# Linear attention and two channel mixers on one core: four weight clamps moved to GpSimd, bonus sums and low parts of four tiles moved to TensorE

## The chip, the cores and the metric

The kernel runs on one core of a Trainium2 chip. The metric is device time in microseconds (us), the median over runs. Trace times count from the first instruction of one profiled execution. The engines are named as in the profile: PE (TensorE matmul), PEld (its weight load), DVE (VectorE), ACT (ScalarE), POOL (GpSimd), SP (SyncE, which issues the DMAs).

## The reference

Three layers follow each other. All inputs and outputs are float32.

```python
# 1. linear attention with decay, batch 4, 8 heads, 768 steps, head size 48
for t in range(S):
    cur = einsum('bhd,bhe->bhde', u * k[t], v[t])
    y[t] = einsum('bhd,bhde->bhe', r[t], state + cur)
    state = w * state + einsum('bhd,bhe->bhde', k[t], v[t])
# 2. x = y as [4, 768, 384]; gated mixer with a 3-tap convolution along the sequence
h = relu(x @ w_in)                      # 384 -> 1024
c = conv3(h, conv_w);  x1 = (h * sigmoid(c)) @ w_out
# 3. residual mixer
out = x1 + relu(layernorm(x1) * g_ln @ w_ch1) @ w_ch2   # 384 -> 1536 -> 384
```

The term with `u` is the bonus: for one position and head it is the sum over the head's 48 entries of r·u·k, times v.

## The kernel before, in words

**Tiles.** The sequence is cut into tiles of 128 positions: 24 tiles (`NT`), 6 per batch entry. Attention works tile by tile. Within a tile the decayed r and k (`rk`, transposed, scaled in place by the tables `trk`) give a score matrix per head (`dot_products`, eight matmuls into two PSUM tiles `dps`); its strict upper triangle, with the bonus on the diagonal, is `aT`; `products` multiplies `aT` with v and adds the contribution of the carried state (`sbd`), into the PSUM tile `yps`. The state is carried by `state_sum` (PE, from the scaled keys `kks`, into PSUM `pst`) and `state_update` (DVE and ACT).

**Split numbers.** Matmuls of the mixers take each float32 operand as a high part (`xh`, rounded to fp32r by an ACT copy) and a low part (`xl`, the rest), and add three products: high·high, high·low, low·high (`mm3`, `down`). The weights are split on the chip as well: 22 weight jobs (`wjob`), each of which loads a block, takes |w| on ACT, clamps it (`magnitude`), decodes it with a shift and two bit operations on DVE (`decode`), rounds the high part on ACT and subtracts on DVE for the low part. Jobs 0 to 9 are `w_in` and `w_out`, which the first mixer needs; jobs 0 to 2 and 4 to 6 are 512 wide, the others 768. The clamp of a job is issued one job ahead (`ahead`), just behind the second bit operation of the job before.

**Three kinds of tiles.** Tiles 0 to 3 (`EARLY`) run in `startup`, ahead of all mixer work, in an order written out by hand and interleaved with weight jobs (`wdo`). Tiles 0 to 5 (`LIGHT`) go through `light_tile`: the bonus sums come from PE (z = scaled r times scaled k on DVE, four matmuls with the small matrix `ub` into `pa8`, an ACT copy to `a8`), are multiplied with v on POOL (`va`) and added by PE. Tiles 4 and 5 also take the low part from PE: `yps` minus `xh` by one matmul with a negated identity (`minus`), then an ACT copy. Tiles 6 to 23 use the other form: the bonus from the untransposed k and r by a multiply (`av`) and a reduce on DVE (`a8`), eight ACT activations that write diagonals into `aT`, two predicated copies on DVE that put the scores above the diagonal, and the low part by a DVE subtract straight after the high part. For this form the keys are scaled with two tables at once (`decayed_k`, 768 wide: decay and bonus); the light form scales with one (384 wide).

**Order.** `attention` is a generator whose steps are called from the first mixer's loop (`after1`, at slots listed in `STEPS`); each tile is itself a generator, advanced by `go_on`. In the usual round of tile n one step holds the state sum of n, its update and the first segment of tile n+1 (scaling, bonus); the next holds products of n and then the scores of n+1. PE runs strictly in the order written. On DVE, ACT, POOL and SP the instructions issued through `vo`, `ao`, `go` and `so` are kept behind the instruction written just before them on that engine, and all others are placed by a planner that simulates the program. In `startup` everything on these engines goes through the ordered forms, so that each engine runs it exactly as written. All attention PSUM tiles with tag `pa` (`dps`, `pa8`, `yps`, `pst`) share three buffers; a tile that finds none free waits for a reader to finish.

The change touches `magnitude`'s caller, `load_rows`, `decayed_k`, `attn_tile`, `startup` and `attention`.

Of the kernel before, what the change touches and what calls it, by code (L numbers as in the profile page):

```python
# [8 lines left out]
F32 = mybir.dt.float32  # L9
F32R = mybir.dt.float32r  # L10
I32 = mybir.dt.int32
AF = mybir.ActivationFunctionType
ALU = mybir.AluOpType
AX = mybir.AxisListType

B, H, S, D = 4, 8, 768, 48
DM = H * D
# [5 lines left out]
C = 128  # L23
# [9 lines left out]
NP = H // 2  # L33
PR = 112
# [2 lines left out]
EARLY = 4  # L37
HAND = 9
LIGHT = 6
STEPS = (2, 4, 6, 8, 10, 12, 15), (1, 3, 4, 6, 7, 9, 10, 12, 14, 16)  # L40
GC = 16
GE = 4
# [8 lines left out]
def body(ctx, tc, r, k, v, w, u, w_in, conv_w, w_out, g_ln, w_ch1, w_ch2, rkT, krv, small, out):  # L51
    nc = tc.nc
# [4 lines left out]
    ap = ctx.enter_context(tc.tile_pool(name="ap", bufs=2))  # L57
# [4 lines left out]
    ps_a = ctx.enter_context(tc.tile_pool(name="ps_a", bufs=3, space=PS))  # L62
    dram = ctx.enter_context(tc.tile_pool(name="dram", bufs=1, space=bass.MemoryType.DRAM))

    v_ = nc.vector
    a_ = nc.scalar
# [12 lines left out]
    pe = InOrder(nc.tensor)  # L79
    vo = InOrder(nc.vector)  # L80
    ao = InOrder(nc.scalar)
    so = InOrder(nc.sync)
    go = InOrder(nc.gpsimd)
# [3 lines left out]
    ident = tables_[:, 0:128]  # L87
    trk = tables_[0:PR, 128:128 + 2 * NP * C].rearrange("x (a p c) -> x a p c", a=2, p=NP)
    tr, tkd = trk[:, 0], trk[:, 1]
    o = 128 + 2 * NP * C  # L90
# [31 lines left out]
    def magnitude(st, n, engine=go):  # L122

        t = ap.tile([128, WN], F32, tag="wd", name="wdec", bufs=2)[:, 0:n]
        ao.activation(out=t, in_=words(st, n)[1].bitcast(F32), func=AF.Abs)
        engine.tensor_scalar(out=t, in0=t, scalar1=W_MIN, scalar2=W_MAX, op0=ALU.max, op1=ALU.min)
        return t
# [14 lines left out]
    def wjob(src, n, hi, lo, scale=None):  # L142

        st, mag = [], []

        def load():
            st.append(io.tile([128, 2 * WN], I32, tag="st" if me >= 4 else "first", name="st", bufs=3 if me >= 4 else 4))
            dst = st[0][:, 0:2 * n]
            if len(src.shape) == 3:
                dst = dst.rearrange("p (a n) -> p a n", a=src.shape[1])  # L150
            so.dma_start(out=dst, in_=src.bitcast(I32))

        def ahead():
            if not mag:
                mag.append(magnitude(st[0], n, vo if me < 10 else go))

        def steps():
            ahead()
            t = mag[0]
            yield from decode(st[0], n, t)  # L160
            if me + 1 < min(len(wjobs), w_loaded[0]):
                wjobs[me + 1][2]()
            if len(src.shape) == 3:
                t = t.rearrange("p (a n) -> p a n", a=src.shape[1])
            kw = {} if scale is None else {"scale": gl[:, scale:scale + 1]}
            ao.activation(out=hi, in_=t, func=AF.Copy, **kw)
            yield
            if scale is None:
                vo.tensor_tensor(out=lo, in0=t, in1=hi.bitcast(F32), op=ALU.subtract)
            else:  # L170
                vo.scalar_tensor_tensor(out=lo, in0=t, scalar=kw["scale"], in1=hi.bitcast(F32),
                                        op0=ALU.mult, op1=ALU.subtract)
        me = len(wjobs)
        wjobs.append((load, steps(), ahead))
        return len(wjobs) - 1

# [34 lines left out]
    def wdo(count=1, last=None):  # L211

        for _ in range(count):
            while w_done[0] < (len(wjobs) if last is None else last + 1):
                wload(w_done[0] + 3)
                if next(wjobs[w_done[0]][1], "end") != "end":
                    break
                w_done[0] += 1
# [21 lines left out]
                     rv[:, DM:].rearrange("x (h d) -> x h d", h=H), rv)  # L240

    def load_rows(n, s_, rv):
        c0 = DM if n < LIGHT else 0
        s_.dma_start(out=rv[:, c0:], in_=krv[n, :, DM + c0:])

    xT = {}
# [5 lines left out]

    def decayed_k(n):

        if n < LIGHT:
            vo.tensor_tensor(out=kks[:, n % 2, 0, :, 0:D], in0=loaded[n][1], in1=tku[:, 0], op=ALU.mult)
            return
        inputs(n).tensor_tensor(out=kks[:, n % 2, :, :, 0:D], in0=loaded[n][1].unsqueeze(1).to_broadcast([128, 2, H, D]), in1=tku,
                         op=ALU.mult)
# [29 lines left out]
    def halos(n, xh, xl):  # L289
        i, j = n % TPB, n // TT  # L290
        g_ = vo if n < EARLY else nc.gpsimd
        for t, e in ((xh, 0), (xl, 1)):
            if i == 0:
                g_.memset(t[:, :, 0:1].bitcast(F32), 0.0)
            if i == TPB - 1:
                g_.memset(t[:, :, T + 1:T + 2].bitcast(F32), 0.0)
            if n % TT == 0 and i > 0:
                g_.tensor_copy(out=xT[j - 1][e][:, :, T + 1:T + 2], in_=t[:, :, 1:2].bitcast(F32))
                g_.tensor_copy(out=t[:, :, 0:1], in_=xT[j - 1][e][:, :, T:T + 1].bitcast(F32))
# [19 lines left out]
    def light_tile(n, rk, vt, py, py_tag):  # L319
# [45 lines left out]
        finished[0] = n  # L365
        yield

    def attn_tile(n):
        b, i = divmod(n, TPB)
        rk, _, rt, vt, _ = loaded[n]  # L370
        py, py_tag = (ps_c, "acc") if n < EARLY else (ps_a, "pa")

        rT, kT = rk[:, 0], rk[:, 1]
        vo.tensor_tensor(out=rk, in0=rk, in1=trk, op=ALU.mult)
        if n < LIGHT:
            yield from light_tile(n, rk, vt, py, py_tag)
            return
        av = ap.tile([128, H, D], F32, tag="av", name="av", bufs=2)
        v_.tensor_tensor(out=av, in0=kks[:, n % 2, 1, :, 0:D], in1=rt, op=ALU.mult)
        a8 = sp.tile([128, H, 1], F32, tag="a8", name="a8", bufs=2)  # L380
        v_.tensor_reduce(out=a8.rearrange("x (q p) o -> x q (p o)", q=2), in_=av.rearrange("x (p q) d -> x q p d", q=2),
                         axis=AX.X, op=ALU.add)
        aT = ap.tile([128, 2, NP, C], F32, tag="aT", name="aT", bufs=2)
        for h in range(H):
            a_.activation(out=aT[:, h // NP, h % NP, :], in_=ident, func=AF.Copy, scale=a8[:, h, :])
        yield

        dps = dot_products(rT, kT)
        for q in range(2):
            v_.copy_predicated(out=aT[:, q], mask=later.bitcast(I32).unsqueeze(1).to_broadcast([128, NP, C]), data=dps[q])  # L390
        yield

        yps = py.tile([128, KT, C], F32, tag=py_tag, name="yps")
        products(n, yps, rT, vt, aT)
        j = n // TT
        xh, xl = xT[j] if j in xT else new_xT(j)
        sl = slice(1 + (n % TT) * C, 1 + (n % TT) * C + C)
        a_.activation(out=xh[:, :, sl], in_=yps, func=AF.Copy)
        v_.tensor_tensor(out=xl[:, :, sl], in0=yps, in1=xh[:, :, sl].bitcast(F32), op=ALU.subtract)
        load_tile(n + 3)  # L400
        if n + 2 < NT:
            decayed_k(n + 2)
        halos(n, xh, xl)
        finished[0] = n
        yield
# [3 lines left out]
    def state_sum(n):  # L409
        vt = loaded[n][3]  # L410
        if n % TPB != TPB - 1:
            pst = sums[n] = ps_a.tile([128, NP, D], F32, tag="pa", name="pst")
            for h in range(H):
                q0 = 64 * (h % 2)
                pe.matmul(pst[q0:q0 + 64, h // 2, :], lhsT=kks[:, n % 2, 0, h, :], rhs=vt[:, h, 0:D], start=True,
                          stop=True)
# [18 lines left out]
    def startup():  # L435

        tiles = {n: attn_tile(n) for n in range(EARLY + 1)}

        def on(n):
            next(tiles[n], None)  # L440

        decayed = decayed_k
        on(0), decayed(0), on(0)
        on(1), state_sum(0), state_update(0), decayed(1), on(1), state_sum(1)
        wdo(1)
        on(0), on(2), state_update(1), decayed(2)
        wdo(2)
        on(2), state_sum(2), on(0)
        wdo(1)
        on(1), on(3), state_update(2), decayed(3)  # L450
        wdo(2)
        on(3), state_sum(3), on(1)
        wdo(2)
        on(2), state_update(3)
        wdo(3)
        on(2), on(3)
        wdo(1)
        on(3)
        wdo(1)
        on(4), decayed(4)  # L460
        wdo(3)
        return tiles

    def attention(tiles):

        def go_on(n):
            if 0 <= n < NT:
                next(tiles.setdefault(n, attn_tile(n)), None)

        n = EARLY  # L470
        load_tile(n + 2)
        decayed_k(n + 1)
        go_on(n)
        yield
        for n in range(EARLY, NT):
            state_sum(n)
            state_update(n)
            go_on(n - 1)
            if n != LIGHT - 1:
                go_on(n + 1)  # L480
            yield
            go_on(n)
            if n == LIGHT - 1:
                yield
                go_on(n)
                go_on(n + 1)
                yield
            go_on(n + 1)
            yield

    def split_T(x, n, hi, lo, c0):
# [456 lines left out]
```

## Time and profile before

| | us |
|---|---|
| median of three runs | 653.33 (652.41 to 654.55) |
| the profiled execution | 653.91 |
| its span, first to last instruction | 652.2 |
| PE busy | 627.9 |
| DVE busy | 421.7 |
| ACT busy | 300.8 |
| POOL busy | 81.2 |

The profiled execution lasts 1.7 us longer than its span, and is 0.6 us above the median. Busy time is the time in which an engine had an instruction running. PE is busy nearly all the span, but its clock is not always granted in full, and DVE has its work mostly in the first half.

### The profile page before, as it was taken

The page shows a single profiled execution, that of the slowest core. Times are in us where ns is not written, and L with a number is a line of the kernel's source. Part 1 is how long each engine was busy: PE and PEld are TensorE (multiplying, and loading weights), DVE is VectorE, ACT ScalarE, POOL GpSimd, SP SyncE. Part 2 cuts the span into 40 slices and gives each one's busy share as a digit, 9 for nine tenths or more (in the row PEclk, how much of TensorE's full clock was granted, in tenths as well). Part 3 has the DMA queues.
Part 4 walks back from the last instruction along what each step waited for, and adds up shares of the span by engine and source line. Part 5 has one row for each costly group of instructions (what it writes and reads, how often), then busy time and mean ns, then how long its engine had stood idle before and what let it go on. Part 6 is the DMA issues. An engine that isn't in the chain of part 4 may idle for free.

```text
span 652.2 us, 11821 instructions
## 1 busy us (share of the span) xinstructions
PE 627.9 (96%) x4803; PEld 572.3 (88%) x4803; DVE 421.7 (65%) x793; ACT 300.8 (46%) x658; POOL 81.2 (12%) x108
## 2 busy tenths in 40 slices
PE   8969879999999999999999999999999999999996
PEld 5768868889999999999999999999999999999995
DVE  6989999999989999968978834314213422422111
ACT  3447677687687877766755511211211211211110
POOL 6312010110020001002115501001000100100000
PEclk8867989999999999999999999999999999999999
DMA  8934644444253524012125103002002001100001
GB/s 231 309 107 156 211 146 125 125 133 159 71 174 118 162 83 137 18 47 88 52 82 171 60 0 98 1 0 98 1 0 83 16 0 50 50 0 19 31 0 54
DMA packets 25296, 56.52 MB, mean 87 GB/s; under 512 B 2961, under 2 KB 15378, under 8 KB 25234
## 3 DMA queue, kind: packets, MB, share of 16 engines
q1 hardware_dynamic: 25234, 55.68, 27.1%
q8 instruction: 40, 0.66, 0.4%
q14 instruction: 22, 0.18, 0.1%
HBM read 46.24 MB, written 9.44 MB: 85 GB/s over the span
## 4 chain that ended last, share of the span: by engine, by line
PE 84%; DVE 10%; ACT 2%; issue 1%; DMA 1%; POOL 1%; SPq 0%; DVEq 0%; ACTq 0%; POOLq 0%
PE acc L77 36%; PE psm L77 36%; PE yps L77 5%; PE dps L77 4%; DVE wdec L77 3%; DVE c L541 2%; PE pst L77 2%; PE pxt L77 1%; DVE rk L77 1%; DMA x1b<-x_dram 1%; DVE c L522 1%; PE pa L77 1%; DVE gl L528 1%; DVE kks L77 0%; POOL tables L762 0%
## 5 line engine op out<-in xcount | busy, mean ns | idle before, releaser
L555 DVE SCALAR_TENSOR_TENSOR rl<-psm,rh 128x512 fp32r<-128x512 f32 x72 | 49.6, 689 | 136.0 <-ACT rh L554 132.5
L554 ACT ACTIVATE rh<-psm 128x512 fp32r<-128x512 f32 x72 | 43.1, 599 | 199.6 <-PE psm L77 199.5
L77 PE MATMUL acc<-c2h,rh 128*128 128x384 f32 x288 | 97.0, 337 | 0.0
L77 PE MATMUL acc<-c2l,rh 128*128 128x384 f32 x288 | 97.0, 337 | 0.0
L77 PE MATMUL acc<-c2h,rl 128*128 128x384 f32 x288 | 96.9, 336 | 0.0
L77 PE MATMUL psm<-xnh,c1h 128*128 128x512 f32 x216 | 86.6, 401 | 0.0
L77 PE MATMUL psm<-xnh,c1l 128*128 128x512 f32 x216 | 84.9, 393 | 0.0
L77 PE MATMUL psm<-xnl,c1h 128*128 128x512 f32 x216 | 84.7, 392 | 0.0
L541 DVE SCALAR_TENSOR_TENSOR c<-h,tables,c 128x384 f32<-128x384 f32 x128 | 78.5, 617 | 8.0 <-ACT c L539 7.5
L77 PE MATMUL psm<-xh,wih 128*128 128x386 f32 x192 | 69.8, 364 | 4.4 <-DVE xl L77 4.4
L77 PE MATMUL acc<-woh,gl 128*128 128x384 f32 x192 | 65.3, 340 | 4.4 <-DVE gl L528 4.4
L77 PE MATMUL acc<-woh,gh 128*128 128x384 f32 x192 | 67.4, 351 | 0.4 <-ACT gh L527 0.4
L77 PE MATMUL psm<-xl,wih 128*128 128x386 f32 x192 | 67.1, 350 | 0.0
L77 PE MATMUL psm<-xh,wil 128*128 128x386 f32 x192 | 66.9, 348 | 0.0
L77 PE MATMUL acc<-wol,gh 128*128 128x384 f32 x192 | 65.3, 340 | 0.0
L77 PEld LDWEIGHTS acc<-c2l,rh 128*128 128x128 f32 x288 | 54.0, 188 | 3.0
L77 PEld LDWEIGHTS acc<-c2h,rh 128*128 128x128 f32 x288 | 54.1, 188 | 2.8
L77 PEld LDWEIGHTS acc<-c2h,rl 128*128 128x128 f32 x288 | 54.0, 188 | 0.0
L77 PEld LDWEIGHTS psm<-xnh,c1l 128*128 128x128 f32 x216 | 40.6, 188 | 9.3
L77 POOL TENSOR_SCALAR wdec<-wdec 128x768 f32<-128x768 f32 (+1 forms) x13 | 35.7, 2749 | 103.4 <-ACT wdec L77 76.3
L77 PEld LDWEIGHTS psm<-xnl,c1h 128*128 128x128 f32 x216 | 40.6, 188 | 6.1
L77 PEld LDWEIGHTS psm<-xnh,c1h 128*128 128x128 f32 x216 | 40.6, 188 | 6.1
(132 smaller groups left out, 1107.9 us busy)
## 6 DMA issues: line engine op xcount, KB each, us to landing
rk<-in_rkT_dram SPq DMA_DIRECT2D x24, 448.0 KB, 4.5
st<-in_moe_w_ch_dram SPq DMA_DIRECT2D x12, 768.0 KB, 4.6
rv<-in_krv_dram SPq DMA_DIRECT2D x18, 448.0 KB, 4.7
kt<-in_krv_dram SPq DMA_DIRECT2D x24, 192.0 KB, 4.5
x_dram<-x SPq DMA_DIRECT2D x24, 192.0 KB, 1.9
x1b<-x_dram SPq DMA_DIRECT2D x24, 192.0 KB, 3.3
out_dram<-x1b SPq DMA_DIRECT2D x24, 192.0 KB, 2.0
st<-in_moe_w_in_dram SPq DMA_DIRECT2D x6, 512.0 KB, 9.4
```

Of the source, the lines that this page charges most:

```text
L77: return lambda *args, **kw: tc.keep_in_program_order(op(*args, **kw))
L522: v_.tensor_tensor(out=st["c"], in0=st["h"][:, 1:T + 1], in1=st["c"], op=ALU.mult)
L528: v_.tensor_tensor(out=st["gl"], in0=st["c"], in1=st["gh"].bitcast(F32), op=ALU.subtract)
L541: v_.scalar_tensor_tensor(out=c, in0=h[:, o:o + T], scalar=cw[:, tap, f:f + 1], in1=c, op0=ALU.mult, op1=ALU.add)
L554: a_.activation(out=gh[:, 0:cols], in_=ps[:, 0:cols], func=AF.Relu)
L555: v_.scalar_tensor_tensor(out=gl_[:, 0:cols], in0=ps[:, 0:cols], scalar=0.0, in1=gh[:, 0:cols].bitcast(F32), op0=ALU.max, op1=ALU.subtract)
```

## The change

Five things are changed.

- The clamps of weight jobs 6, 7, 8 and 9 are issued on POOL (`go`) and not on DVE (`vo`). Jobs 10 to 21 had theirs on POOL already.
- For tiles 6 to 9 (`LIGHT <= n < MID`) the bonus sums are formed as in the light tiles: z on DVE in the tile's first segment, and at the head of its second segment four matmuls into `pa8` and an ACT copy to `a8` (`bonus`). The eight diagonals on ACT follow there, ahead of the scores. The multiply and the reduce on DVE are gone for these tiles.
- Their low parts come from PE and ACT (`minus`), in a segment of their own which `attention` calls behind the second segment of tile n+1. Tile loads and key scaling stay where they were.
- Their keys are scaled with one table, and their untransposed r is no longer loaded (192 KB a tile less).
- In `startup`, the third segment of tile 0 (products, high part) and the first segment of tile 2 (scaling, z) stand ahead of the first `wdo(1)` (|w|, clamp and shift of job 0), and not behind it.

```diff
+MID = 10
@@ wjob
-                mag.append(magnitude(st[0], n, vo if me < 10 else go))
+                mag.append(magnitude(st[0], n, vo if me < 6 else go))
@@ load_rows
-        c0 = DM if n < LIGHT else 0
+        c0 = DM if n < MID else 0
@@ decayed_k
-        if n < LIGHT:
+        if n < MID:
             vo.tensor_tensor(out=kks[:, n % 2, 0, :, 0:D], in0=loaded[n][1], in1=tku[:, 0], op=ALU.mult)
             return
@@
+    def bonus(bank, z, a8):
+        pa8 = bank[:, 0:H]
+        for p in range(NP):
+            pe.matmul(pa8[:, 2 * p:2 * p + 2], lhsT=z[:, p, :], rhs=ub[:, 2 * p:2 * p + 2], start=True, stop=True)
+        nc.scalar.activation(out=a8.rearrange("x h o -> x (h o)"), in_=pa8, func=AF.Copy)
+
@@ attn_tile
-        av = ap.tile([128, H, D], F32, tag="av", name="av", bufs=2)
-        v_.tensor_tensor(out=av, in0=kks[:, n % 2, 1, :, 0:D], in1=rt, op=ALU.mult)
         a8 = sp.tile([128, H, 1], F32, tag="a8", name="a8", bufs=2)
-        v_.tensor_reduce(out=a8.rearrange("x (q p) o -> x q (p o)", q=2), in_=av.rearrange("x (p q) d -> x q p d", q=2),
-                         axis=AX.X, op=ALU.add)
         aT = ap.tile([128, 2, NP, C], F32, tag="aT", name="aT", bufs=2)
-        for h in range(H):
-            a_.activation(out=aT[:, h // NP, h % NP, :], in_=ident, func=AF.Copy, scale=a8[:, h, :])
-        yield
+
+        def diagonals(of):
+            for q in range(2):
+                for p in range(NP):
+                    a_.activation(out=aT[:, q, p, :], in_=ident, func=AF.Copy, scale=a8[:, of(q, p), :])
+
+        if n < MID:
+            z = ap.tile([PR, NP, C], F32, tag="z", name="z", bufs=2)
+            vo.tensor_tensor(out=z, in0=rT, in1=kT, op=ALU.mult)
+            yield
+            bonus(ps_a.tile([128, 512], F32, tag="pa", name="pa8"), z, a8)
+            diagonals(lambda q, p: 2 * p + q)
+        else:
...
+            yield
 
         dps = dot_products(rT, kT)
@@
         a_.activation(out=xh[:, :, sl], in_=yps, func=AF.Copy)
-        v_.tensor_tensor(out=xl[:, :, sl], in0=yps, in1=xh[:, :, sl].bitcast(F32), op=ALU.subtract)
         load_tile(n + 3)
         if n + 2 < NT:
             decayed_k(n + 2)
+        if n < MID:
+            yield
+            pe.matmul(yps, lhsT=minus, rhs=xh[:, :, sl], start=False, stop=True, skip_group_check=True)
+            a_.activation(out=xl[:, :, sl], in_=yps, func=AF.Copy)
+        else:
+            v_.tensor_tensor(out=xl[:, :, sl], in0=yps, in1=xh[:, :, sl].bitcast(F32), op=ALU.subtract)
         halos(n, xh, xl)
@@ startup
         on(1), state_sum(0), state_update(0), decayed(1), on(1), state_sum(1)
+        on(0), on(2)
         wdo(1)
-        on(0), on(2), state_update(1), decayed(2)
+        state_update(1), decayed(2)
@@ attention
             go_on(n + 1)
+            if LIGHT <= n < MID:
+                go_on(n)
             yield
```

In the branch for the other tiles (the line of dots) the multiply, the reduce and the diagonals stand as before.

## Rows read from the trace of the kernel before

**Rows 1.** Busy time per stretch: PE, PEld, DVE, ACT, POOL, granted clock, DMA.

```profile
13.20:16.09 2.89, 2.89 (x26) 2.71 (x24) 0.01 (x1) 1.94 (x4) 2.56 (x4) 0.50 1.08 295
16.09:40.10 24.01, 19.10 (x311) 15.21 (x310) 22.26 (x43) 11.57 (x25) 6.44 (x11) 0.86 0.82 250
40.10:51.90 11.80, 11.21 (x59) 9.96 (x59) 9.00 (x19) 5.10 (x11) 2.29 (x4) 0.50 0.49 152
51.90:94.00 42.10, 35.70 (x309) 33.33 (x308) 42.07 (x70) 31.59 (x69) 7.04 (x6) 0.91 0.51 164
94.00:126.00 32.00, 30.25 (x407) 26.84 (x407) 30.14 (x55) 22.90 (x62) 1.81 (x4) 1.00 0.48 141
126.00:320.00 194.00, 191.72 (x1938) 180.14 (x1937) 176.31 (x321) 147.90 (x349) 21.59 (x25) 1.00 0.32 104
```

**Rows 2.** The same view, of two shorter stretches of the saturated part.

```profile
86.00:90.00 4.00, 0.70 (x4) 0.38 (x4) 4.00 (x8) 3.95 (x12) 0.00 (x0) 1.00 0.21 25
90.00:94.00 4.00, 4.00 (x15) 4.00 (x14) 4.00 (x8) 2.33 (x7) 0.00 (x0) 0.57 0.88 309
```

**Rows 3.** Waits of PE from 40 to 330 us: total, times, longest.

```profile
PE psm L77 <- DVE xl L77: 4.4, 1, 4.4
PE acc L77 <- DVE gl L528: 4.4, 2, 3.3
PE dps L77 <- ACT c L539: 1.9, 1, 1.9
```

**Rows 4.** DVE in order of time at the start: start, duration, instruction, idle before.

```profile
16.09 0.99 DVE L77 TENSOR_SCALAR wdec<-wdec 128x512 f32<-128x512 f32 x2 [2.89 <-ACT wdec L77]
17.00 1.22 DVE L77 TENSOR_TENSOR rk<-rk,tables 112x1024 f32<-112x1024 f32 x1
...
18.93 0.35 DVE L77 TENSOR_TENSOR sn<-pst,sw 112x192 f32<-112x192 f32 x1
...
35.08 0.56 DVE L77 TENSOR_SCALAR wdec<-wdec 128x768 f32<-128x768 f32 x1 [1.29 <-ACT wdec L77]
...
39.34 0.55 DVE L77 TENSOR_TENSOR xl<-yps,xh 128x384 fp32r<-128x384 f32 x1
```

**Rows 5.** ACT in order of time at the start.

```profile
15.38 0.68 ACT L77 ACTIVATE wdec<-st 128x512 f32<-128x512 f32 x1
19.65 0.49 ACT L77 ACTIVATE xh<-yps 128x384 fp32r<-128x384 f32 x1 [3.60 <-PE yps L77]
20.04 0.73 ACT L77 ACTIVATE sbds<-sn 48x192 f32<-48x192 f32 x2
```

**Rows 6.** DVE groups by shape from 51 to 95 us: count, busy, mean ns.

```profile
L77 DVE TENSOR_SCALAR wdec<-wdec 128x768 f32<-128x768 f32 x3 | 2.3, 759 | 0.0
L77 DVE TENSOR_TENSOR kks<-kt,tables 128x768 f32<-128x768 f32 x2 | 1.9, 944 | 0.0
L379 DVE TENSOR_TENSOR av<-kks,rv 128x384 f32<-128x384 f32 x2 | 1.1, 544 | 0.0
L381 DVE TENSOR_REDUCE a<-av 128x8 f32<-128x384 f32 x2 | 1.1, 538 | 0.0
L77 DVE TENSOR_TENSOR z<-rk 112x512 f32<-112x512 f32 x1 | 0.7, 681 | 0.0
```

**Rows 7.** PE in order of time: bonus matmuls and low part of light tiles.

```profile
58.38 1.02 PE L77 MATMUL pa<-ub,z 112*128 112x2 f32 x8 [0.74 <-ACT aT L335]
...
73.11 0.34 PE L77 MATMUL yps<-xh,minus 128*128 128x384 f32 x1
73.30 0.34 PE L77 MATMUL psm<-xh,wih 128*128 128x386 f32 x1
```

**Rows 8.** ACT in order of time: a copy to a8, eight diagonals of one tile.

```profile
59.76 0.16 ACT L338 ACTIVATE a<-pa 128x8 f32<-128x8 f32 x1
...
86.20 2.45 ACT L385 ACTIVATE aT<-tables,a 128x128 f32<-128x128 f32 x8
```

**Rows 9.** A clamp on POOL, and DVE in the same time.

```profile
82.48 2.77 POOL L77 TENSOR_SCALAR wdec<-wdec 128x768 f32<-128x768 f32 x1 [19.95 <-ACT wdec L77]
...
82.76 0.96 DVE L522 TENSOR_TENSOR c<-h,c 128x384 f32<-128x384 f32 x1
83.64 1.13 DVE L541 SCALAR_TENSOR_TENSOR c<-h,tables,c 128x384 f32<-128x384 f32 x2
84.70 0.94 DVE L77 SCALAR_TENSOR_TENSOR wdec<-st,wdec 128x768 int32<-128x768 int32 x1
```

More of the change, by code (lines that the diff above doesn't have):

```diff
@@ L377, in attn_tile @@
             return
-        av = ap.tile([128, H, D], F32, tag="av", name="av", bufs=2)
-        v_.tensor_tensor(out=av, in0=kks[:, n % 2, 1, :, 0:D], in1=rt, op=ALU.mult)
         a8 = sp.tile([128, H, 1], F32, tag="a8", name="a8", bufs=2)
-        v_.tensor_reduce(out=a8.rearrange("x (q p) o -> x q (p o)", q=2), in_=av.rearrange("x (p q) d -> x q p d", q=2),
-                         axis=AX.X, op=ALU.add)
         aT = ap.tile([128, 2, NP, C], F32, tag="aT", name="aT", bufs=2)
-        for h in range(H):
-            a_.activation(out=aT[:, h // NP, h % NP, :], in_=ident, func=AF.Copy, scale=a8[:, h, :])
-        yield
+        def diagonals(of):
[9 more added lines that the diff above has]
+        else:
+            av = ap.tile([128, H, D], F32, tag="av", name="av", bufs=2)
+            v_.tensor_tensor(out=av, in0=kks[:, n % 2, 1, :, 0:D], in1=rt, op=ALU.mult)
+            v_.tensor_reduce(out=a8.rearrange("x (q p) o -> x q (p o)", q=2),
+                             in_=av.rearrange("x (p q) d -> x q p d", q=2), axis=AX.X, op=ALU.add)
+            diagonals(lambda q, p: q * NP + p)
+            yield
         dps = dot_products(rT, kT)
```

## The prediction

> **What bounds the kernel now.** I read the busy time by stretch first, because the share over the whole span (PE 96%) mixes stages with different limits; then PE's waits, then DVE and ACT in order of time where PE stood still. The reader is to see four stages in [rows 1]. Until 40.1 us PE only does the first four tiles, and DVE, with 22.26 us of work in the 24.01 us from 16.09, sets the pace: PE's first mixer matmul waits 4.4 us for the last low part [rows 3], which DVE starts at 39.34 [rows 4]. From 40.1 to 51.9 PE works at half clock (0.50, the 1.2 GHz level) and DVE has slack. From 51.9 to 94 DVE is full, 42.07 of 42.10 us, while PE has 35.70: this is the stage where DVE work is worth time. Within it PE waits 1.9 us ahead of scores (put down to ACT, but the scaled `rk` that they read is only just finished on DVE) and 3.3 us for one `gl` [rows 3]; from 86 to 90 PE is busy 0.70 of 4 us, and behind that pause its clock is 0.57 over four microseconds [rows 2]. From 94 to 126 PE has 30.25 of 32 us, so only 1.75 us are left to win, and from 126 to 320 it has 191.72 of 194 [rows 1]. Nothing after that is touched.
>
> So the same edit has two prices: DVE work taken away before 94 us shortens the run, PE work added after 94 us lengthens it by its full length.
>
> **The change, part by part.**
>
> *Startup.* Nothing can be passed here: DVE, ACT and PE run it as written. Before, ACT takes |w| of job 0 at 15.38, right behind the bonus copy of tile 1, and then waits 3.60 us for PE to finish `yps` of tile 0, whose copy starts at 19.65 [rows 5]. DVE idles 2.89 us until the clamp at 16.09 [rows 4]. After, scaling and z of tile 2 fill that idle: from 17.00 to 18.93 they take 1.93 us [rows 4]. But the third segment of tile 0 moves along, and its high-part copy now stands ahead of |w| on ACT. PE's order up to there is unchanged, so that copy still starts at 19.65; the next ACT instruction started at 20.04 [rows 5], so |w| runs from 20.04 to 20.72 and DVE's clamp starts at about 20.75. Queued behind the clamp on DVE: shift, state sum and everything else up to the last low part. Clamp and shift take 16.09 to 17.00, so `sn` starts at 20.75 + 0.91 = 21.66 where it was 18.93: **2.7 us later**, and DVE is the pace of this stage. What can absorb it is one idle of 1.29 us at 35.08 [rows 4], if the ACT and PE work it waits for slips less than DVE. Bounds: +1.4 (2.7 less 1.29) to +3.0; I take +2.4, nearer to the full shift, because that idle waits for a chain that itself starts with a DVE result. No DMA changes place: neither segment issues one, and job 0 is already loaded.
>
> *DVE relief from 51.9 to 94.* Removed by [rows 6]: the wide clamps of jobs 7, 8 and 9, 3 × 0.759 = 2.3 us; the narrower one of job 6, estimated at 0.4 from its two thirds of the width; half of the key scaling of tiles 6 and 7, 2 × (0.944 − 0.544) = 0.8, with the 384-wide multiply as the price of what stays; multiply and reduce of tiles 6 and 7, 2 × (0.544 + 0.538) = 2.2. Added: one z before the stall at 86 us, 0.7. Net 5.0 us of busy time. Instructions overlap a little at their ends, and PE (35.70 + 1.0 for the bonus of tile 6) would be nearly full too, so not all comes through: I take −3.8, with −2.0 and −5.0 as ends. If the pause at 86 to 90 shrinks to a fraction, the slow clock behind it goes too: 0.57 over 4 us means about 3.4 us at half rate, so 1.7 us lost; I take −1.6, ends 0 and −1.7.
>
> *The clamps on POOL.* POOL has 7.04 us of work in these 42 [rows 1], one clamp takes 2.77 us [rows 9]. |w| of a job is taken one job ahead, so DVE's shift should find the clamp done. Where it doesn't (job 7, whose clamp meets the masking and `va` of tile 5 on POOL), shift and bit operations of the job are behind it on DVE; that is up to one clamp, and is in the −2.0 end. While the clamp at 82.48 ran, DVE's next multiply took 0.96 where the mean of its kind is 0.544 [rows 6, 9], and the two instructions behind it ran on in the same 2.77 us: 0.4 us at most, four times 1.6, again inside that end.
>
> The Trainium skill, page "SBUF — State Buffer", section "Who interferes with whom", says that a DVE instruction with two SBUF inputs contends with a GpSimd instruction that reads SBUF, and that the loser of the shared ports blocks until the other ends. By that rule each clamp could hold DVE for its whole length. The row shows a slowing of 0.4 us and no block [rows 9].
>
> *PE after 94.* Bonus matmuls of tiles 7, 8 and 9 at about 1.0 us [rows 7] (that of tile 6 falls into PE's idle time before 94), and four low-part matmuls at 0.19, the distance from one to the next instruction [rows 7]: 3.0 + 0.8 = +3.8. Of the idle 1.75 us, where scores wait for DVE, relief saves perhaps 1.2: −1.2 (ends 0 and −1.75).
>
> *A new wait on PSUM.* The low part now needs `yps` of tile n until after the scores of n+1. There are three buffers: `yps`, `pa8` and the first `dps` take them, so the second `dps` waits for the ACT copy that empties `pa8`. Queued behind it on PE are the rest of the scores, the low-part matmul and the mixer. The near row is the light tile 5, where `pa8` itself waited 0.74 us for ACT to empty a score buffer [rows 7]; the copy takes 0.16 [rows 8]. It happens for tiles 7, 8 and 9. I take 0.6 each, +1.8; below 0.3 each it can hardly be (copy and hand-over), and 1.5 each if ACT, busy 22.90 of 32 us there [rows 1], has long work ahead: +0.9 to +4.5. The eight diagonals, 2.45 us on ACT [rows 8], start only behind this copy, one segment later than before; products come two steps on, so I cost this at nothing, with the slow rival below if that cover is gone.
>
> *At nothing:* the ACT copies for the low part (slack on ACT), the shorter loads (DMA share is 0.48 there), the halo copies on POOL behind them (their mixer starts later). The segments keep their place among SP's loads.
>
> **Sum.** +2.4 − 3.8 − 1.6 + 3.8 − 1.2 + 1.8 = **+1.4**. On the profiled 653.9 this is 655.3; the profiled run lies 0.6 above the median, so as a median 653.3 + 1.4 = 654.7.
>
> **Rivals.**
> *Faster.* DVE relief comes through in full and PSUM waits stay at their low end: +2.0 − 5.0 − 1.7 + 3.8 − 1.75 + 0.9 = −1.75, and with the startup shift at its low end −2.35: about 651. For it: DVE has no idle at all from 51.9 to 94. Against: PE has only 6.4 us of idle there and must take in a bonus. It would also come about if the startup move filled 1.9 us of DVE's idle and |w| of job 0 were not held: +1.4 − 2.4 − 1.9 = −2.9, 650.4. Chance together 0.24.
> *Slower.* One mechanism: PE stops at the second `dps` until ACT has done the copy. Should the planner place that copy behind ACT work that itself waits for DVE, each of three tiles loses 2 us and not 0.6, and diagonals, masks and products slip with it: 1.4 + 4.2 = +5.6, 659. It decides from about 1.1 us a tile, where the sum passes 0.3%. For it: ACT's planned order rests on simulated times, and at 86 to 90 ACT is full. Against: the copy is ready early. Chance 0.26.
> *Clamps block DVE* (the mechanism of [rows 9], at full length): 4 × 2.77 less 1.6 already counted = up to 9.5 us on DVE before 94, about half of it hidden: 654.7 + 5 to + 9, some 662. The page named above states this rule; the trace of before speaks against it. Chance 0.04.
> *It doesn't do what it says*, DVE freed but PE held by other waits at the same places: 654.7 + 3.8 = 658.5; counted with the slower one.
>
> **How the numbers follow.** Forecast 0.46, faster 0.24, slower 0.26, block 0.04. About 0.3% (2.0 us) is what a measurement of this kernel can tell from no change: 651.4 to 655.3. The forecast's own range, 652.3 to 657, lies mostly within and partly above. So faster 0.24, same 0.43, slower 0.33. The range that leaves out 2 in 10 reaches from the faster rival to the slower one: 650.2 to 659.2.
>
> **What would show it.** Startup: first mixer matmul at 42 to 43 us, not 40.1; DVE idle of over 5 us before the clamp of job 0, |w| behind `xh` on ACT. Relief: PE's busy time between its first full-clock stretch and the end of tile 7 above 35.7 of 42.1, no wait of 3.3 us for `gl`, no slow clock behind it. After: `dps` waiting for the `a8` copy three times. I would be wrong if the first mixer matmul came at 40 or sooner, or if a clock drop moved elsewhere and stayed.

## The result, and the profile after

The changed kernel takes 661.07 us (median of six runs, 658.94 to 662.63) where the kernel before, run beside it, takes 654.63 (652.41 to 656.21). The ratio is 1.0102, 95% interval 1.0083 to 1.0122: 6.7 us slower by the ratio (6.4 between the medians), where 1.4 us slower was forecast and 659.2 was the upper end. The profiled execution lasts 661.05, its span is 659.3.

The stretches of [rows 1], same view of the changed kernel (PE, PEld, DVE, ACT, POOL busy, granted clock, DMA). They are cut at the same times, though the changed kernel comes to the same work up to 5 us later:

```profile
16.09:40.10 24.01, 19.12 (x304) 16.04 (x295) 18.05 (x34) 11.54 (x24) 7.45 (x12) 0.84 0.71 239
40.10:51.90 11.80, 9.45 (x63) 8.51 (x64) 10.71 (x22) 4.26 (x9) 2.47 (x4) 0.71 0.28 86
51.90:94.00 42.10, 34.71 (x277) 32.86 (x277) 40.37 (x61) 29.99 (x60) 21.25 (x9) 0.80 0.56 170
94.00:126.00 32.00, 31.96 (x379) 28.80 (x378) 26.80 (x47) 24.73 (x70) 0.33 (x2) 1.00 0.32 99
126.00:320.00 194.00, 192.38 (x1994) 179.44 (x1993) 175.25 (x318) 146.67 (x349) 23.73 (x28) 1.00 0.34 106
```

Two readings. From 94 to 126 PE has no idle time left: 31.96 of 32 us, against 30.25 [rows 1]. From 51.9 to 94, where the change was to give time to PE, PE has less busy time than before (34.71 against 35.70), and at a lower granted clock (0.80 against 0.91), although DVE was relieved. PE's waits up to 340 us, beside [rows 3]:

```profile
PE psm L78 <- DVE xl L78: 4.4, 1, 4.4
PE pa L78 <- DVE z L78: 4.4, 2, 3.9
PE dps L78 <- ACT h L565: 3.0, 1, 3.0
PE dps L78 <- DVE rk L78: 1.6, 1, 1.6
PE acc L78 <- DVE gl L555: 1.5, 2, 1.2
```

The wait of 3.3 us for `gl` is gone; one of 3.9 us for z, the new input of the bonus matmuls, stands in its place, and one of 3.0 us ahead of the scores of tile 5 is new. PE in order of time at the first of these:

```profile
82.12 0.33 PE L78 MATMUL psm<-xh,wil 128*128 128x386 f32 x1
86.37 1.84 PE L78 MATMUL pa<-ub,z 112*128 112x2 f32 x8 [3.92 <-DVE z L78]
88.14 2.08 PE L78 MATMUL dps<-rk 48*128 48x128 f32 x16
```

Behind the pause the clock drops, as it did behind the old one [rows 2]: the bonus takes 1.84 us where it takes 1.02 at full clock [rows 7], the scores 2.08 where the same form takes 1.16 in the later tiles. DVE in order of time says why z is late:

```profile
81.97 1.22 DVE L78 TENSOR_TENSOR rk<-rk,tables 112x1024 f32<-112x1024 f32 x1
83.11 0.95 DVE L78 SCALAR_TENSOR_TENSOR wdec<-st,wdec 128x768 int32<-128x768 int32 x1
83.97 1.18 DVE L568 SCALAR_TENSOR_TENSOR c<-h,tables,c 128x384 f32<-128x384 f32 x1
85.08 0.55 DVE L549 TENSOR_TENSOR c<-h,c 128x384 f32<-128x384 f32 x1
85.55 0.68 DVE L78 TENSOR_TENSOR z<-rk 112x512 f32<-112x512 f32 x1
```

The scaled `rk` itself ends only at 83.2, and the planner put three instructions between it and z. None of these five has any idle time ahead of it: DVE is still the pace.

The other wait, ahead of the scores of tile 5, is where this execution falls behind. PE in the kernel before and, below it, in the changed one:

```profile
56.48 1.16 PE L77 MATMUL dps<-rk 48*128 48x128 f32 x16
58.28 2.08 PE L78 MATMUL dps<-rk 48*128 48x128 f32 x16 [2.98 <-ACT h L565]
```

The h that the wait is put down to was done at 57.80; the scaled `rk`, which the scores read, at 58.18:

```profile
56.96 1.22 DVE L78 TENSOR_TENSOR rk<-rk,tables 112x1024 f32<-112x1024 f32 x1
```

In the kernel before, that scaling starts at 54.48, so DVE is 2.5 us late, about as late as the startup left it (2.3 us, below). PE was not late: its clock was back at 1.00 from 48 us, where it was 0.50 up to 51.9 before [rows 1], and it ended the products of tile 4 1.2 us earlier than before. So it had to wait for `rk`, and the time at half clock behind the wait is longer. From 60 to 70 us, before and after:

```profile
60.00:70.00 10.00, 10.00 (x99) 9.55 (x99) 10.00 (x16) 6.71 (x12) 2.53 (x3) 0.86 0.31 90
60.00:70.00 10.00, 9.50 (x40) 9.23 (x39) 10.00 (x15) 6.59 (x14) 9.72 (x5) 0.59 0.27 80
```

At the products of tile 5 PE is 4.3 us behind the kernel before (72.45 against 68.19), at those of tile 6 4.0 us (98.31 against 94.27). The pause for z, with the slow clock behind it, costs no more than the pause that it replaces.

The startup, beside [rows 4] and [rows 5], ACT first and then DVE:

```profile
18.22 0.49 ACT L78 ACTIVATE xh<-yps 128x384 fp32r<-128x384 f32 x1 [3.90 <-PE yps L78]
18.74 0.67 ACT L78 ACTIVATE wdec<-st 128x512 f32<-128x512 f32 x1
```

```profile
13.35 1.84 DVE L78 TENSOR_TENSOR rk<-rk,tables 112x1024 f32<-112x1024 f32 x1
...
19.44 0.89 DVE L78 TENSOR_SCALAR wdec<-wdec 128x512 f32<-128x512 f32 x2 [3.21 <-ACT wdec L78]
20.24 0.35 DVE L78 TENSOR_TENSOR sn<-pst,sw 112x192 f32<-112x192 f32 x1
...
37.41 0.56 DVE L78 TENSOR_SCALAR wdec<-wdec 128x768 f32<-128x768 f32 x1 [2.44 <-ACT wdec L78]
```

|w| now stands behind the high-part copy, the clamp starts at 19.44 and not at 16.09, and PE's first mixer matmul comes at 42.45, not 40.11: 2.3 us later. Only 1.3 us of that are there at `sn` (20.24 against 18.93 [rows 4]). The rest comes behind it: from 27 to 35 us the granted clock is 0.57 where it is 0.79 in the kernel before, PE is later with a `yps` (copied at 35.32, not 32.96), and DVE's idle time of 1.29 us [rows 4] grows to 2.44.

Three points that both kernels pass place the loss. First mixer matmul: 40.11 before, 42.45 after (+2.3). First output of the mixer's first block stored: 101.70 and 106.90, so another +2.9 between. First load behind the last block of the first mixer: 292.15 and 297.49, +0.1. The remaining 1.8 of the 7.1 us that the span grew lie behind that load.

### The profile page after: what moved, and what is told of

The parts are those of the page before. It is cut to its first block, busy times and chain, and to the rows that moved or that the text cites. A ratio compares the mean times of both kernels' runs of the same rounds, so it can differ in the third digit from the quotient of the medians.

```text
span 659.3 us, 11881 instructions
## 1 busy us (share of the span) xinstructions
PE 634.9 (96%) x4839; PEld 578.2 (88%) x4839; DVE 421.3 (64%) x781; ACT 303.9 (46%) x666; POOL 96.5 (15%) x112
## 4 chain that ended last, share of the span: by engine, by line
PE 88%; DVE 7%; DMA 2%; ACT 1%; issue 1%; POOL 0%; SPq 0%
PE acc L78 37%; PE psm L78 36%; PE yps L78 5%; PE dps L78 4%; DVE wdec L78 2%; PE pa L78 2%; PE pst L78 2%; PE pxt L78 1%; DMA kt<-in_krv_dram 1%; DVE rk L78 1%; DMA x1b<-x_dram 1%; DVE c L568 1%; DVE c L549 0%; ACT wdec L78 0%; POOL tables L789 0%
## 5 line engine op out<-in xcount | busy, mean ns | idle before, releaser
L568 DVE SCALAR_TENSOR_TENSOR c<-h,tables,c 128x384 f32<-128x384 f32 x128 | 80.6, 634 | 9.7 <-ACT c L566 9.0
L78 PE MATMUL psm<-xh,wih 128*128 128x386 f32 x192 | 68.4, 357 | 4.4 <-DVE xl L78 4.4
L78 POOL TENSOR_SCALAR wdec<-wdec 128x768 f32<-128x768 f32 (+2 forms) x17 | 50.3, 2961 | 95.1 <-ACT wdec L78 66.2
```

The costliest lines, as they stand in the source:

```text
L78: return lambda *args, **kw: tc.keep_in_program_order(op(*args, **kw))
L568: v_.scalar_tensor_tensor(out=c, in0=h[:, o:o + T], scalar=cw[:, tap, f:f + 1], in1=c, op0=ALU.mult, op1=ALU.add)
```

## The experiments

Two theories are compared throughout. **A**: each part has its own price (the startup slip, the clamps' relief and their contention, PE's added work), and the prices add. **B**: DVE's pace and the order that the planner makes anew for each kernel decide what the parts bring, so that freed DVE time reappears as another wait. Ratios are to the kernel before, run beside each kernel; 0.001 is 0.65 us. PE's order is the one written in all of them.

### The three parts, alone and in pairs

The parts of the diff: the startup move, the clamps on POOL, the new form of tiles 6 to 9.

```diff
 start
+        on(0), on(2)
         wdo(1)
-        on(0), on(2), state_update(1), decayed(2)
+        state_update(1), decayed(2)
 clamps
-                mag.append(magnitude(st[0], n, vo if me < 10 else go))
+                mag.append(magnitude(st[0], n, vo if me < 6 else go))
 tiles
+MID = 10
...
```

> The kernel before with the startup move alone. Theory: |w| of job 0 stands behind the high part of tile 0 on ACT, DVE idles about 3 us before its clamp in a new place and the whole chain to the first mixer matmul slips: that matmul at 42.5 us and not 40.1, +2.3 us in the end (about 657 beside 654.6). Rival: the slip is taken up later by PE's waits for DVE, under +0.7 us at the end.

> The kernel before with the four clamps on POOL alone. Theory (contention): while a clamp runs on POOL, DVE instructions with two inputs in SBUF take about 0.4 us longer and the clamp itself 3 to 5 us instead of 2.8, so that the 2.7 us taken from DVE come back as lost time and tile 5's masking on POOL is late: 0 to +2 us. Rival (relief): DVE is full in this stage and 2.7 us fewer there give -1.5 to -2.5 us.

> The kernel before with bonus sums and low parts of tiles 6 to 9 on PE and keys with one table, but clamps and startup as before. Theory (z): the bonus matmuls of tile 6 head its scores on PE and wait for z, which the planner puts two or three DVE instructions behind the scaling; a pause of about 4 us with a slow clock behind it stays, and no relief arrives: +1 to +3 us. Rival (relief): pauses at 78 to 90 us shrink, -2 to -4 us.

> The changed kernel with the startup order of the kernel before. Theory (new order): the parts don't add up, since each makes the planner order DVE anew; without the startup slip of 2.3 us this is at +1 to +4.5 us beside the kernel before. Rival (additive): clamps +3 and tiles +2 give +5 us.

> The changed kernel with the four clamps back on DVE. Theory (contention matters): without the clamps on POOL, tile 5's masking isn't held up and DVE isn't slowed; 1 to 3 us less than the changed kernel, +3.5 to +5.5 us beside the kernel before. Rival (additive): startup +6.6 and tiles +2 give +8.6 us. Third (startup order alone decides): +6 to +7 us.

> The startup move and the four clamps on POOL, without the part on the tiles. If each part has its own cost, the ratio is the product of the two alone, about 1.0147 (664 us). If the costs of the parts come mainly from the order that the planner makes anew for each kernel, they do not add: anywhere from 1.005 to 1.011, and the first mixer matmul is still 2 to 3 us late.

| parts | ratio | 95% interval |
|---|---|---|
| start | 1.0101 | 1.0068 to 1.0134 |
| clamps | 1.0046 | 1.0028 to 1.0063 |
| tiles | 1.0032 | 1.0011 to 1.0052 |
| start and clamps | 1.0061 | 1.0039 to 1.0084 |
| start and tiles | 1.0083 | 1.0055 to 1.0111 |
| clamps and tiles | 1.0031 | 1.0011 to 1.0052 |
| all three | 1.0102 | 1.0083 to 1.0122 |

No part alone is a gain, and they do not add: the three alone sum to +0.0179, together they cost 0.0102, and start with clamps costs less than start alone, by 0.0040, which is as much as the two intervals combined leave open. Averaged over the four pairs of kernels that differ by one part only, the startup move costs (1.01 + 0.15 + 0.51 + 0.71)% / 4 = 0.6%, 3.9 us; the clamps 0.4 us and the tiles 0.7 us, each to about 1 us, so that neither of the last two can be told from nothing.

Why do they not add? The moved startup lines alone give the engines another order: read from the traces by the form of the instruction, 119 of DVE's 793 places and 88 of ACT's 658 hold another instruction than in the kernel before, where the edit itself moves 6 and 2 (start_held, below). In the kernel with start alone PE has a wait that no other kernel here has:

```profile
94.60 0.69 PE L77 MATMUL acc<-woh,gh 128*128 128x384 f32 x1 [5.89 <-ACT gh L528]
```

ACT had the sixteen diagonals of two tiles to do ahead of that `gh`:

```profile
85.61 2.46 ACT L385 ACTIVATE aT<-tables,a 128x128 f32<-128x128 f32 x8
...
89.16 2.16 ACT L385 ACTIVATE aT<-tables,a 128x128 f32<-128x128 f32 x7 [0.67 <-DVE a L381]
...
94.04 0.51 ACT L528 ACTIVATE gh<-c 128x384 fp32r<-128x384 f32 x1
```

### The startup slip without the new order

The same move, with DVE, ACT and POOL held, from tile 4 on, in the order they have in the kernel before (order-only dependencies, no waits). `HELD` lists, for each engine, the numbers of the instructions in that order.

```diff
...
+    by_name = {i.name: i for i in nc.cur_bb.bb.instructions}
+    for order in HELD:
+        for first, then in zip(order, order[1:]):
+            tc.add_manual_dep(by_name[f"I-{then}"], f"I-{first}",
+                              mybir.DependencyInfo(mybir.DependencyClass.NoSync, mybir.DependencyReason.DATA), reason="held")
```

> The startup move alone, but from tile 4 on every instruction of DVE, ACT and POOL is held in the order that the planner gave the kernel before, by added order-only dependencies. Theory (new order): the startup slip itself is worth +2.3 to +3.4 us, and the rest of the 6.6 us of the startup move alone comes from the order that the planner makes anew for DVE and ACT in the mixer stage; held, the end is at +2 to +3.5 us (about 657). Rival (lateness): the slip meets PE's clock and waits in a worse phase whatever the order; +5 to +7 us stay.

1.0049 (1.0032 to 1.0066), 3.2 us. Its first mixer matmul comes at 42.55, 2.4 us late, and its span is 2.6 us longer than before. So the slip alone is 2.4 to 3.2 us, and of the 6.6 us that start costs, about half is the new order: 3.4 us, 1.0 to 5.8 with the two intervals combined. The profiled executions agree. In start, 3.4 of the 8.1 us that its span is longer lie ahead of the first mixer matmul (43.46) and 4.8 behind it; in start_held, 2.4 of 2.6 lie ahead and 0.2 behind.

### Which of the two moved segments costs it

```diff
+        on(2)
         wdo(1)
-        on(0), on(2), state_update(1), decayed(2)
+        on(0), state_update(1), decayed(2)
```

First in the kernel before (start2), then in the changed kernel (after2): only scaling and z of tile 2 go ahead, the third segment of tile 0 stays behind |w|, clamp and shift. The lines shown are those of start2; after2 ends at the same ones.

> The kernel before with only scaling and z of tile 2 ahead of the first weight step, products and high part of tile 0 behind it as they were. Theory: |w| of job 0 is not held on ACT, the two instructions (1.9 us) fill DVE's idle 2.9 us, the first mixer matmul comes at about 38.3 and not 40.1: -1 to -1.9 us at the end. Rival: PE and ACT set the pace of this stage as well, under 0.7 us either way.

> The changed kernel with the third segment of tile 0 put back behind the |w|, clamp and shift of job 0; only the first segment of tile 2 stands ahead. Theory: the startup cost is the clamp's wait for the high-part copy, which waits for PE at half clock; without it |w| runs at 14 to 16 us as before, the first mixer matmul comes at 39 to 41, and the ratio is that of the changed kernel without the startup part or lower, 1.000 to 1.004. Rival: scaling and z of tile 2 ahead of the clamp cost as much by themselves in this kernel: ratio 1.008 to 1.011.

start2: 1.0003 (0.9982 to 1.0025). The clamp follows at 16.30 with no idle time of DVE ahead of it, and the first mixer matmul comes at 39.29, but the 1 to 1.9 us that were expected do not show at the end. after2: 1.0036 (1.0017 to 1.0055), against 1.0102 for the changed kernel: the one segment left behind gives back 0.0066, 4.3 us, and what stays is what clamps and tiles cost without any startup move (1.0031). ACT of after2 takes |w| before the copy again, and PE has the first mixer matmul at 39.48:

```profile
14.68 0.67 ACT L78 ACTIVATE wdec<-st 128x512 f32<-128x512 f32 x1 [0.48 <-DMA st<-in_moe_w_in_dram]
18.43 0.49 ACT L78 ACTIVATE xh<-yps 128x384 fp32r<-128x384 f32 x1 [3.08 <-PE yps L78]
```

So the cost comes with the segment of tile 0: behind it the clamp of job 0 waits for the high-part copy, and with that for PE. The planner's order differs as well between these two kernels (61 of 781 places on DVE), so the 4.3 us are not this wait alone; in start2 the order is nearly that of before (4 of 793 places). How long the clamp waits depends on PE's clock, which falls to 0.50 somewhere between 10 and 30 us, not at the same place in each execution. In the execution of start it falls between 10 and 12 and stays low beyond 20; ACT's copy starts at 21.10 and DVE idles 6 us:

```profile
22.32 0.89 DVE L77 TENSOR_SCALAR wdec<-wdec 128x512 f32<-128x512 f32 x2 [6.03 <-ACT wdec L77]
```

In that of the kernel with start and clamps, whose startup code is the same, it stays at 1.00 until 18 us:

```profile
16.80 0.49 ACT L77 ACTIVATE xh<-yps 128x384 fp32r<-128x384 f32 x1 [2.05 <-PE yps L77]
17.32 0.67 ACT L77 ACTIVATE wdec<-st 128x512 f32<-128x512 f32 x1
```

Its first mixer matmul comes at 39.18, and the startup has no slip there. Over the profiled executions of all kernels:

| order in startup | executions | copy of tile 0 starts | first mixer matmul | mean |
|---|---|---|---|---|
| as before, or only tile 2 ahead | 11 | 16.71 to 21.44 | 39.02 to 41.17 | 39.9 |
| tile 0 and tile 2 ahead | 6 | 16.80 to 21.10 | 39.18 to 43.95 | 42.2 |

In the old order the latest copy is 4.7 us behind the earliest, and the latest mixer start 2.2 us; in the new order both are over 4 us. The mean slip is 2.3 us; the six values lie from 0.7 us ahead of the other mean to 4.0 behind it.

### What the clamps bring and what they cost

clamps_held is the kernel with the clamps on POOL, with DVE and ACT held in the order of the kernel before; noclamps holds the same order and leaves the four clamps out, on every engine, so it computes less.

```diff
 noclamps
+        if engine is not None:
-        engine.tensor_scalar(out=t, in0=t, scalar1=W_MIN, scalar2=W_MAX, op0=ALU.max, op1=ALU.min)
+            engine.tensor_scalar(out=t, in0=t, scalar1=W_MIN, scalar2=W_MAX, op0=ALU.max, op1=ALU.min)
...
-                mag.append(magnitude(st[0], n, vo if me < 10 else go))
+                mag.append(magnitude(st[0], n, vo if me < 6 else None if me < 10 else go))
```

> The four clamps on POOL alone, with DVE (less the clamps) and ACT held in the order of the kernel before from tile 4 on. Theory (new order): the clamps themselves cost nothing, the +3 us of the clamps alone come from the new order; held, -2 to 0 us. Rival (contention): DVE's two-input instructions and the clamps slow each other, and masking of tile 5 is late behind a clamp on POOL; +1 to +3 us stay.

> The kernel before without the clamps of weight jobs 6 to 9 on any engine (left out of the computation, so its time is that of less work), all else on VectorE and ScalarE held in the order of before, as in the kernel with the clamps on GpSimd and the order held (ratio 1.0026). If VectorE's work before 94 us sets the pace, 2.7 us less of it bring 2 to 3 us: ratio 0.995 to 0.997, and the difference of 4 to 5 us to the held kernel is the price of the clamps on GpSimd (contention and waits). If VectorE is not the pace, the ratio is 0.999 to 1.002, and the clamps on GpSimd cost less than 2 us.

clamps_held 1.0026 (1.0011 to 1.0040), noclamps 0.9979 (0.9964 to 0.9993), between its two expectations. So 2.7 us less work on DVE bring 1.4 us (0.5 to 2.4), about half of it, and the same clamps on POOL cost 0.0047, 3.1 us (1.7 to 4.4, with the two intervals combined): more than the relief is worth. The order is the same instruction for instruction, so the price can be read off. POOL in clamps_held:

```profile
51.95 1.92 POOL L81 TENSOR_SCALAR wdec<-wdec 128x512 f32<-128x512 f32 x1 [2.05 <-DVE c L545]
58.17 5.31 POOL L81 TENSOR_SCALAR wdec<-wdec 128x768 f32<-128x768 f32 x1 [4.30 <-ACT wdec L81]
63.43 2.04 POOL L340 TENSOR_SCALAR_AFFINE_SELECT aT<-aT 128x512 f32<-128x512 f32 x2
...
66.55 3.07 POOL L81 TENSOR_SCALAR wdec<-wdec 128x768 f32<-128x768 f32 x1
73.26 3.06 POOL L81 TENSOR_SCALAR wdec<-wdec 128x768 f32<-128x768 f32 x1 [3.65 <-ACT wdec L81]
```

DVE in clamps_held, one instruction beside each of the four clamps:

```profile
51.33 1.65 DVE L545 SCALAR_TENSOR_TENSOR c<-h,tables,c 128x384 f32<-128x384 f32 x2 [0.74 <-ACT c L543]
...
60.76 1.18 DVE L545 SCALAR_TENSOR_TENSOR c<-h,tables,c 128x384 f32<-128x384 f32 x1
...
66.91 1.17 DVE L532 TENSOR_TENSOR gl<-c,gh 128x384 fp32r<-128x384 f32 x1
...
73.61 1.58 DVE L81 SCALAR_TENSOR_TENSOR wdec<-st,wdec 128x768 int32<-128x768 int32 x1
```

The first, third and fourth of these in noclamps, and between them one of the second's form with nothing on POOL beside it:

```profile
50.69 1.27 DVE L546 SCALAR_TENSOR_TENSOR c<-h,tables,c 128x384 f32<-128x384 f32 x2 [0.74 <-ACT c L544]
...
64.80 0.60 DVE L546 SCALAR_TENSOR_TENSOR c<-h,tables,c 128x384 f32<-128x384 f32 x1
65.33 0.55 DVE L533 TENSOR_TENSOR gl<-c,gh 128x384 fp32r<-128x384 f32 x1
...
71.40 0.95 DVE L81 SCALAR_TENSOR_TENSOR wdec<-st,wdec 128x768 int32<-128x768 int32 x1
```

Each clamp holds up one DVE instruction, by 0.38, 0.58, 0.62 and 0.63 us; those around it run at their usual length. That is 2.2 us given back of 2.7. (The two masks and `va` of tile 5 do the same to three instructions in both kernels.) POOL loses as well: a clamp that took 2.77 us in [rows 9] takes 5.31, and the masking of tile 5 starts behind it at 63.43, where it starts at 58.55 in noclamps. The remaining 0.9 us of the 3.1 lie within its uncertainty.

### z of tile 6 earlier

The kernel's own order is held on DVE, ACT and POOL, and one instruction is moved: z of tile 6 right behind the scaling of its `rk`. The edit is the loop shown above, with the kernel's own lists. tiles_z does it in the kernel with tiles alone, after_z in the changed kernel.

> The same single move in the kernel that has only the part on tiles 6 to 9: z of tile 6 right behind rk of tile 6. Theory: PE's wait of 4.14 us ahead of the bonus of tile 6 falls to about 1.9, and the half clock from 82 to 88 goes with it: 2 to 4 us less than that kernel, ratio 0.997 to 1.000. Rival: the wait moves on, ratio 1.002 to 1.004 as without the move.

> The changed kernel with its own order on DVE, ACT and POOL held, and one instruction moved: z of tile 6 (84 to 86 us) stands right behind the scaling of rk of tile 6 and not three DVE instructions later. Theory: the 3.92 us that PE waits for z, and the half clock behind that wait, are lost time. Then z ends near 83.9 and not 86.2, PE's bonus matmuls start near 84.0, the wait is about 1.5 us, and the run is 2 to 4 us shorter than the changed kernel: ratio to the kernel before 1.004 to 1.007. Rival: DVE is the pace of this stage and PE meets the same lateness one wait later (for the masked scores or the next gl); then the wait here shrinks by 2.4 us, another grows by as much, and the ratio stays at 1.009 to 1.011.

tiles_z 1.0045 (1.0026 to 1.0063) where tiles has 1.0032; after_z 1.0094 (1.0071 to 1.0117) where the changed kernel has 1.0102. No gain. The wait itself fell as worked out; PE in tiles:

```profile
81.31 1.18 PE L78 MATMUL pa<-ub,z 112*128 112x2 f32 x8 [4.14 <-DVE z L78]
```

and in tiles_z:

```profile
78.85 1.02 PE L83 MATMUL pa<-ub,z 112*128 112x2 f32 x8 [1.94 <-DVE z L83]
...
93.02 1.84 PE L83 MATMUL pa<-ub,z 112*128 112x2 f32 x8 [3.29 <-DVE z L83]
```

2.2 us were saved at tile 6, and 3.3 us are waited at tile 7, with the half clock (the 1.84) behind that wait. In tiles no wait stands there. In after_z PE still waits 3.83 us ahead of tile 6, since the scaling of `rk` was late too. The theory that this one wait is the loss falls: with it shortened, PE meets DVE's lateness at the next operand.

### The new form for tile 6 alone

`MID = 7` and not 10, without startup move and clamps; then with the first segment of tile 2 ahead (as start2).

> The kernel before with the new form (bonus sums and low part from TensorE, one key table) for tile 6 alone; tiles 7 to 9 as before, start and clamps as before. It keeps nearly all relief of DVE that lies before 94 us except half a key scaling, and leaves out three bonuses and three low-part matmuls on PE, 3.6 us, which come after 94. By the prediction (work added to PE there costs its full length) it is 3 to 4 us faster than with tiles 6 to 9: ratio 0.996 to 0.998. Rival (that work is paid for by waits of PE for scores that it saves): no faster than with tiles 6 to 9, ratio 1.001 to 1.004.

> The kernel before with the new form for tile 6 alone and only the first segment of tile 2 moved ahead. Sum of the two alone (1.0014 and 1.0003): 1.002. If the order that the planner makes decides, it lies anywhere from 0.998 to 1.005.

tile6 1.0014 (1.0000 to 1.0028), tile6_start2 1.0016 (0.9995 to 1.0036). Against tiles (1.0032), tile6 leaves 3.6 us of work on PE undone and is 1.2 us faster, with 1.6 us of uncertainty. That is less than 3.6, as if part of what PE gets after 94 us were paid for by waits that it no longer has. But tile6 also has 1.5 us more work on DVE before 94, for tile 7: key scaling (0.41 more), multiply (0.55) and reduce (0.54), of which the expectation counts only the first. So this pair alone does not show it; PE's idle time does (next section). None of the kernels with a part of the change beats the kernel before.

## Why the prediction was wrong

*Where the sum failed.* The terms other than the startup add up to −1.0 us (−3.8 − 1.6 + 3.8 − 1.2 + 1.8); the kernel with clamps and tiles measured +2.0 (1.0031). The startup stood at +2.4; its move measured +4.6 on top of that kernel (1.0102 against 1.0031), and 3.9 on average. So two steps failed: the relief of DVE, and the startup move, priced by its slip alone.

*What bounds the kernel*: right. DVE sets the pace until about 94, PE after it; the idle time from 94 to 126 went to nothing.

*Startup, +2.4*: the mechanism (|w| behind the copy, clamp behind |w|) was right, and so was the mean slip: 2.3 over the executions, 2.4 to 3.2 with the order held. That the profiled execution has 2.3 as well is luck. "That copy still starts at 19.65" did not hold: it starts when PE's clock lets it, between 16.7 and 21.4, and the new order hands that to DVE. Here it started at 18.22, so `sn` slipped by 1.3 us and not by 2.7; and the idle time that was to absorb some of the slip grew. What the sum lacked is the rest of the move's cost. One part of it goes through the planner, which ordered DVE and ACT anew, a term that the prediction does not have: about 3.4 us in start alone. In the changed kernel, whose order was new anyway, the move's 4.3 to 4.6 us and the slip of 2.3 are too close, given their uncertainty, to say how much it is.

*DVE relief, −3.8, and the slow clock, −1.6*: this step failed. It counted freed DVE time as freed PE time, at three quarters. For the clamps, the share is about one half (1.4 of 2.7 us; three quarters is within its uncertainty), but the clamps on POOL cost 3.1 us and took it back. The contention was foreseen nearly in its size (0.4 us a clamp, 1.6 for four; measured 0.38 to 0.63, 2.2), but the working left it "inside that end" of the range and did not subtract it from the −3.8. For the tiles, the relief at 86 to 90 did end the wait for `gl`, but the working did not ask what is late next, above all the new operand: z sits on the same full DVE, and PE needs it at the head of the segment, ahead of the scores. The pause stayed (3.92 us), and so did the half clock behind it, so the −1.6 did not come either. What took the place of the relief in the profiled execution is the wait at tile 5: DVE came there with the lateness of the startup, which the relief behind it did not make up: at the scaling for tile 6 it is 3.2 us late (81.97 against 78.82). That is a sign that the prediction names for being wrong, a clock drop that moves elsewhere: from 51.9 to 94 the granted clock is 0.80 and not 0.91.

*PE after 94, +3.8, saved waits, −1.2*: the added work was sized right (the bonus takes 1.05 here), but the saved waits were too small. Idle time of PE fell by 1.71 us from 94 to 126 and by 0.66 from 126 to 320 (32 − 31.96 and 194 − 192.38 against [rows 1]); from the first stored output to the first load behind the first mixer the two kernels differ by 0.1 us, though two bonuses and three low parts were added there, and PE's idle time between these points fell from 2.98 to 0.20 us. The forecast of 1.2 counted idle time only up to 126.

*PSUM wait, +1.8*: too large. PE in the changed kernel, tiles 7 and 8:

```profile
100.31 1.16 PE L78 MATMUL dps<-rk 48*128 48x128 f32 x16
...
109.98 1.68 PE L78 MATMUL dps<-rk 48*128 48x128 f32 x16
```

Only one of the three times does the second score tile wait, 0.5 us within the group of tile 8 (1.68 less 1.16). The slower rival put its chance of 0.26 on this mechanism; a time beyond its 659 came about without it. By its own sum that rival passes 0.3% from about 0.8 us a tile (1.4 + 3 × 0.2 = 2.0), not 1.1.

*Clamps block DVE, 662*: as a total near the result, as a mechanism not. DVE ran on beside each clamp. The Trainium skill, page "SBUF — State Buffer", section "Who interferes with whom", has DVE instructions with two SBUF inputs contend with GpSimd instructions that read SBUF, and the loser block. The trace agrees that the two contend, and shows another price: one DVE instruction beside each clamp is longer by 0.4 to 0.6 us, where a clamp runs 1.9 to 5.3 us.

By places, the 7.1 us of span are 2.3 startup (forecast 2.4), 2.9 from there to the first stored output (forecast: relief of 5.4 against the bonuses of tiles 6 and 7 and a low part, some −3), 0.1 to the end of the first mixer (forecast +3 to +4), and 1.8 behind it (forecast nothing). Of the last, PE's waits for `gl` account for 0.4 (1.5 against 1.1 us behind 292); the rest stays open.

## What to carry to other kernels

Work taken off a saturated engine is worth only what the consumer's next operand from that engine allows: before counting a removed wait, ask when the same engine delivers the operand behind it, the new one above all, and how late that engine already is when it gets there. Filling an idle gap is no gain if the piece moved into it makes the saturated engine wait for a slower one, here DVE for a PE at half clock. And where a planner orders the engines, an edit of a few lines is two edits: price them apart by holding the old order, since in start the new order alone cost about as much as the edit.

## What the runs showed of the hardware

In the two held kernels, each of the GpSimd instructions on large tiles (clamps, masks, `va`) held up about one DVE instruction beside it, by 0.4 to 0.6 us, however long it ran itself: a clamp of 128x768 took 2.77 us at one place and 5.31 at another, with about the same price for DVE (0.4 and 0.6 us). In the startup the granted clock falls to 0.50 at places some 8 us apart in executions of the same startup code (between 10 and 12 us in start, between 18 and 20 in start with clamps), and what that costs is set by who waits for PE behind it.
